# The opening of an attention and FNet kernel: another heads' table for the first batch, work moved to ScalarE and GpSimd, queues reordered

## The chip, the cores and the metric

The kernel runs on one core of one Trainium2 chip. A core has five engines with their own instruction queues: TensorE (PE, whose weight loads are listed apart as PEld), VectorE (DVE), ScalarE (ACT), GpSimd (POOL) and SyncE (SP), which here only issues DMAs. An engine works through its queue in order, and waits in front of an instruction until the semaphores that it needs are there. The metric is the time on the device in microseconds; less is better.

## The reference

Eight batches of 8 heads, 576 tokens and 64 columns a head, all in fp32. First linear attention, then a Fourier mix with an MLP:

```python
q_s = exp(q - max(q, -1)); q_s = q_s / (sum(q_s, -1) + 1e-9)       # softmax over the 64 columns
k_s = exp(k - max(k, 2));  k_s = k_s / (sum(k_s, 2) + 1e-9)        # softmax over the 576 tokens
kv  = einsum('bhsd,bhse->bhde', k_s, v)                            # 64 x 64 a head
x   = einsum('bhsd,bhde->bhse', q_s, kv)  -> (8, 576, 512)         # heads side by side
mixed = real(fft(fft(x, axis=1), axis=2))
u   = x + mixed
un  = (u - mean(u)) / sqrt(var(u) + 1e-6)
out = u + max(un @ w_ch1, 0) @ w_ch2                               # 512 -> 2048 -> 512
```

## The kernel before

The batches are worked one after the other. What this document is about is the opening, batch 0, up to its MLP; batches 1 and up, and the MLP of all of them, are not touched.

**Keys and the heads' table.** The keys come transposed, two heads to a block of 128 rows, so there are four blocks `k00` to `k03` (`first_keys`, from L541). For each: maximum on VectorE (L554), exponential on ScalarE with its sum (L557), four transposes on PE (`turn`, L562), a copy from PSUM on ScalarE (`four`, L565). The last 64 tokens of all blocks are turned together (`last`, L570) and copied by VectorE (`fifth`, L573). `inverse` (L576, L577) takes the reciprocal of the sums. The products with the values (`times`, L586) give one 64x64 block for each head; the two heads of a pair lie one above the other in 128 rows. `scale` (L589) multiplies them with the reciprocals while it copies them from PSUM into `self.pairs[0]`, 128 rows by four pairs by 65 columns; the 65th column is one, and gives the softmax's sum of a query when it is multiplied along.

**Queries.** Batch 0's 576 query rows are split into four tiles of 128 rows, A, B, C and D, whose rows mirror each other in time (so that sums and differences of them are the folded input of a real Fourier transform), and one tile t of the remaining rows (64 of batch 0 and 64 of batch 1). For each tile: maximum by head (L968, VectorE), subtraction (L973, GpSimd for A, B and C, VectorE for D and t), exponential (L977, ScalarE), transposes (L985, PE), a copy from PSUM (L996, or L1006 for t into `self.F`, both ScalarE). For A to D the product with the table is made in `own_times_kv` (L840): sixteen matmuls of 64 rows with 64x65 of the table, whose 65th columns are turned into reciprocals (L862, L864) and multiplied in while VectorE copies the result from PSUM into x (L876). Tile t is normalized before its product (L946, L947, L948, L957, VectorE); GpSimd folds its transposed columns (L1018 to L1026), and `t_times_kv` multiplies them (L840 and L1061): 24 matmuls. ScalarE copies the results out (L1070, L1073), and VectorE folds the tile `g` over columns (L1085, L1087, L1088).

**Folds and transform.** `folded(0)` gives four tiles `eo`: 0 and 1 are sums of x rows, 2 and 3 differences (`tokens`, L1104). `columns` folds them over the features (L1115 and L1116 for the sums, L1110 for the differences), and the differences are combined again (`by`, L1123; `again`, L1129 and L1130). PE multiplies them with cosine tables (`e0`, `e1`: L1217) and sine tables (`e2`, `e3`: L1224), adds g's part (`tails`, L1234); the result is copied out (L1246 to L1250), transformed over the features (L1264, L1267), added to x (L1281 to L1295) and normalized, transposed (L1365), and goes into the MLP, whose first product is L1467.

**What sets the order.** The engines' queues are filled by an order written by hand. `OPENING` is a string of keys and steps (`14.75 t inverse, 14.76 k0 scale`); the steps are issued in the order of the keys, which are no times. Each engine sees its own instructions in that order. `WARM` puts extra matmuls on PE, whose results are not used (key, number, columns; L270). `BY_ACT` names the query tiles whose product ScalarE copies out. The loads of the opening are issued on SyncE in one list (`loads_first`): four blocks of keys, tile t's rows in four loads (L296), two of query rows (L315), `shared_firsts` (L299: four single rows of t, 8 KB, into rows that one of the loads before writes), values (L310, L311), transform tables (L343 to L347), then the weights. PSUM's tiles `two` have three buffers in the opening and `tr` two, taken in turn.

Of the kernel before, what the change touches and what calls it, by code (L numbers as in the profile page):

```python
# [52 lines left out]
HD = D // 2  # L53
NN = HD + 1
# [36 lines left out]
7.25 k01 turn, 7.56 k02 exp, 7.75 k03 max, 8.32 k01 four, 8.51 k02 turn, 8.82 k03 exp, 8.90 A max, 9.50 B max,  # L91
9.58 k02 four, 9.65 A less, 9.77 k0 last, 10.10 k0 inverse, 10.27 k03 turn, 10.42 k0 fifth, 10.69 B less,
10.80 A exp, 11.30 k03 four, 11.84 B exp, 11.85 A turn, 12.20 C max, 12.45 A copy,
12.80 D max, 12.90 C less, 12.95 B turn, 13.00 t max, 13.10 D less, 13.20 t less, 13.55 B copy, 14.00 k00 kv, 14.01 k01 kv, 14.10 C exp, 14.11 C turn, 14.12 D exp, 14.13 t exp, 14.14 C copy,
14.2 k02 kv, 14.3 k03 kv, 14.4 D turn, 14.41 D copy, 14.75 t inverse, 14.76 k0 scale, 14.8 t normal, 15.0 A kv, 15.1 t turn, 15.31 t copy, 15.4 C kv, 15.45 B kv,
18.48 A inverse, 18.50 A out, 18.60 C inverse, 18.61 C out, 18.62 D kv, 18.90 B inverse, 19.01 B out,
19.63 D inverse, 19.70 D out, 20.00 t fold, 20.1 t join, 20.2 t kv, 20.3 t parts, 20.43 tokens0, 20.5 columns0, 20.6 e0,
20.70 tokens1, 20.80 columns1, 20.9 e1, 21.02 roots,
21.1 c0 hi, 21.11 c0 lo, 21.12 c1 hi, 21.13 c1 lo,
21.15 t folds, 21.2 tokens2, 21.3 tokens3, 21.35 columns2, 21.4 columns3, 21.5 by2, 21.6 by3, 21.7 again2, 21.75 e2, 21.76 kept0, 21.8 again3, 21.85 e3, 21.9 tails,  # L100
21.91 c0 shift, 21.92 c0 sign, 21.93 c0 add,
# [37 lines left out]
class _Block:  # L139
    def __init__(self, ctx, tc, q, kT, v, w1, w2, ft, cd, out):  # L140
# [134 lines left out]
    def loads_first(self, fetch):  # L275
# [37 lines left out]
        def queries(i):  # L313
# [4 lines left out]
        order = [lambda: nc.gpsimd.memset(v[0:64, 4, :], 0.0), table, *each(keys), shared, lambda: queries(0), lambda: queries(1),  # L318
                 shared_firsts, lambda: values(0), lambda: values(2), self.tables, *(lambda i=i: fetch(i) for i in range(11))]
        later = [step for _, step in self.keys_to(1) + [(0, self.prepare)] + self.values_to(1, 0)]  # L320
# [219 lines left out]
    def first_keys(self, b):  # L540
# [3 lines left out]
        v = [v[:, :, r * P:(r + 1) * P] for r in range(NR)]  # L544
        copy, box, top = nc.vector.tensor_copy, {}, {}
        rec = self.small.tile([P, NR], F32, tag="kinv", name="kinv", bufs=2)
        steps = {}

# [23 lines left out]
        def fifth():  # L572
            copy(self.fifth[64:], box["last"][64:])  # L573

        def inverse():
            V.tensor_scalar(out=rec[:], in0=rec[:], scalar1=ATT_EPS, scalar2=None, op0=ALU.add)  # L576
            V.reciprocal(rec[:], rec[:])  # L577

        def times(r):
# [20 lines left out]
    def opening(self, fetch, converted):  # L600
# [20 lines left out]
        named("t fold,t join", self.t_fold(shared))  # L621
        named("t kv,t parts,t folds", self.t_times_kv(0))
        for n, it in own.items():
            named(f"{n} max,{n} less,{n} exp", self.q_exp_spread(it, V if n == "D" else None))
            named(f"{n} turn,{n} copy", self.q_turn(it))
            named(f"{n} kv,{n} inverse,{n} out", self.own_times_kv(it, act=n in BY_ACT))
        for name, f in zip(("tokens", "columns", "by", "again"), self.folded(0)):
# [195 lines left out]
    def by_head(self, b, left, turned=False, n=DH + 1, shared=False):  # L823
# [24 lines left out]
        return [(r, t.rearrange("p h (r n) -> p h r n", n=n)) for r, t in parts] + [px]  # L848

    def own_times_kv(self, it, shared=False, act=False):  # L850
        nc, V, (_, b, c, u) = self.nc, self.nc.vector, it
# [179 lines left out]
    def q_times_kv(self, it, turned=False):  # L1031
# [12 lines left out]
        return [(0, times), (1.3, out)]  # L1044

    def t_times_kv(self, b):
        nc, V = self.nc, self.nc.vector
# [34 lines left out]

        def folds():
            g = self.live["g", b]
            V.scalar_tensor_tensor(out=g[:, 1:HD], in0=g[:, D - 1:HD:-1], scalar=self.sign[:, 0:1], in1=g[:, 1:HD],  # L1085
                                   op0=ALU.mult, op1=ALU.add)
            V.tensor_tensor(out=g[:, NN:NN + QD], in0=g[:, 0:QD], in1=g[:, HD:QD:-1], op=ALU.subtract)  # L1087
            V.tensor_tensor(out=g[:, 0:QD], in0=g[:, 0:QD], in1=g[:, HD:QD:-1], op=ALU.add)  # L1088

        return [(0, times), (1.3, copies), (8 if b > 1 else 3, folds)]  # L1090

    def folded(self, b):
# [5 lines left out]
        def tokens_folded(some):  # L1100
            for i in some:
                e, op = ((V if b < 2 else G), ALU.add) if i < 2 else (V, ALU.subtract)
                eo[i] = self.halves()
                e.tensor_tensor(out=eo[i][:, 0:D], in0=self.xpart(b, i % 2, 0), in1=self.xpart(b, i % 2, 1), op=op)  # L1104

        def columns_folded(some):
            for i in some:
                e, op = ((V if b < 2 else G), ALU.add) if i < 2 else (V, ALU.subtract)
                t = eo[i]
                e.tensor_tensor(out=t[:, 1:HD], in0=t[:, 1:HD], in1=t[:, D - 1:HD:-1], op=op)  # L1110
# [883 lines left out]
```

## Time and profile before

| | |
|---|---|
| median of 3 runs | 1006.84 us (1006.43 to 1006.99) |
| the profiled execution, span from the first to the last instruction | 1006.6 us |
| granted TensorE clock, mean | 1.000 |
| matmul busy / span | 995.6 us, 99% |
| VectorE, ScalarE, GpSimd busy | 71%, 49%, 44% |
| DMA moved | 236.37 MB, 235 GB/s |
| first product of batch 0's MLP (L1467) starts at | 42.70 us |

For the profiled execution no time other than its span is given. It stands 0.24 us below the median of the runs. A group in the profile is a source line, an engine and an operation with its tiles; `x8` behind it is a count. A matmul in fp32 shows as two records on PE and two weight loads on PEld, a transpose as one of each. "issue" in the chain is time in which an engine waited for nothing that the profile shows.

### The profile page before, as it was taken

Reading aid. Unit: us, or ns where it says so; the run is one execution under the profiler, and the core shown is the slowest. Engines: PE = TensorE matmul, PEld = TensorE weight load, DVE = VectorE, ACT = ScalarE, POOL = GpSimd, SP = SyncE. Lnnn points to the kernel's source line nnn. Section 1 sums busy time; section 2 is a strip of 40 time slices with the busy share of each in tenths; the row PEclk is TensorE's granted clock in tenths of the full one; section 3 lists DMA queues with packets and bytes.
Section 4 is the critical chain, followed back from the end, with each engine's and each line's share of the span. In section 5 each row is a group of like instructions: output and inputs, shape, how many; then the busy total and the mean of one; then the engine's idle time right before and its main releaser. Section 6 shows DMA issues by size and latency. Waiting matters only on the chain.

```text
span 1006.6 us, 19808 instructions
## 1 busy us (share of the span) xinstructions
PE 995.6 (99%) x7562; PEld 855.7 (85%) x7562; DVE 718.6 (71%) x1356; ACT 493.2 (49%) x1277; POOL 442.9 (44%) x445
## 2 busy tenths in 40 slices
PE   8999999999999999999999999999999999999998
PEld 6844464888888899889988998899889998998897
DVE  6898898666765887588756877688667945685563
ACT  4585642872468228832775177625772342151200
POOL 4263420357535637664655465655646450040000
PEclk9999999999999999999999999999999999999999
DMA  9987499687989666975677577847753765674573
GB/s 300 258 281 245 158 240 346 205 243 226 342 283 272 230 230 219 266 237 210 251 220 242 206 269 237 253 174 270 231 204 135 267 213 200 224 265 172 183 256 132
DMA packets 123559, 236.37 MB, mean 235 GB/s; under 512 B 24184, under 2 KB 88440, under 8 KB 112840
## 3 DMA queue, kind: packets, MB, share of 16 engines
q1 hardware_dynamic: 123096, 234.58, 71.0%
q8 instruction: 60, 0.98, 0.4%
q14 instruction: 35, 0.29, 0.1%
q10 hardware_dynamic: 288, 0.26, 0.1%
q0 software_dynamic: 80, 0.26, 0.1%
HBM read 199.94 MB, written 39.06 MB: 237 GB/s over the span
## 4 chain that ended last, share of the span: by engine, by line
PE 87%; DVE 7%; ACT 3%; DMA 1%; issue 1%; SPq 0%; POOL 0%; DVEq 0%; POOLq 0%
PE bb L1544 16%; PE ba L1544 11%; PE bc L1544 11%; PE bb L1671 10%; PE ba L1671 7%; PE bc L1671 7%; PE bb L1641 5%; PE bc L1479 2%; PE bb L1760 2%; PE two L840 2%; PE one L755 2%; PE two L1207 1%; PE two L1264 1%; PE ba L1479 1%; PE bc L1760 1%; PE ba L1760 1%
## 5 line engine op out<-in xcount | busy, mean ns | idle before, releaser
L1544 PE MATMUL bb<-unT,big 128*128 128x256 f32 x768 | 183.3, 380 | 0.0
L1544 PEld LDWEIGHTS bb<-unT,big 128*128 128x128 f32 x768 | 144.8, 190 | 20.7 <-DVE u L1514 0.7
L1556 ACT ACTIVATE big<-big 128x512 f32<-128x512 f32 x96 | 59.8, 629 | 147.6 <-DVE big L1555 141.0
L1544 PE MATMUL ba<-unT,big 128*128 128x256 f32 x512 | 123.9, 382 | 0.0
L1544 PE MATMUL bc<-unT,big 128*128 128x256 f32 x512 | 121.5, 380 | 0.1
L817 ACT ACTIVATE qT<-q 32x128 f32<-32x128 f32 x384 | 117.9, 307 | 5.9 <-DVE q L807 0.8
L1544 PEld LDWEIGHTS bc<-unT,big 128*128 128x128 f32 x512 | 96.9, 190 | 13.7 <-DVE big L1555 0.5
L1544 PEld LDWEIGHTS ba<-unT,big 128*128 128x128 f32 x512 | 95.5, 190 | 13.9 <-issue 0.5
L1514 DVE TENSOR_TENSOR u<-bb,s 128x512 f32<-128x512 f32 x66 | 45.2, 685 | 85.0 <-PE bb L1544 66.5
L1671 PE MATMUL bb<-big 128*128 128x128 f32 x848 | 103.8, 276 | 0.2 <-DVE u L1678 0.2
L1671 PEld LDWEIGHTS bb<-big 128*128 128x128 f32 x848 | 98.9, 192 | 1.0 <-DVE u L1678 1.0
L1390 POOL COPY unT<-unT 32x256 f32<-32x256 f32 x98 | 42.0, 428 | 90.2 <-DVE unT L1382 85.9
L1621 POOL TENSOR_TENSOR x<-x,big 128x512 f32<-128x512 f32 x45 | 60.9, 1368 | 46.0 <-DVE big L1678 19.7
L1617 DVE TENSOR_TENSOR big<-big 128x512 f32<-128x512 f32 x98 | 79.9, 842 | 0.0
L1671 PE MATMUL ba<-big 128*128 128x128 f32 x640 | 79.0, 276 | 0.0
L1671 PEld LDWEIGHTS ba<-big 128*128 128x128 f32 x640 | 75.0, 192 | 0.8
L1390 ACT COPY unT<-unT 32x256 f32<-32x256 f32 x126 | 50.7, 402 | 31.3 <-DVE unT L1382 29.5
L804 POOL TENSOR_TENSOR q<-q,qm 128x512 f32<-128x512 f32 x24 | 25.8, 1073 | 88.2 <-DVE qm L799 53.1
L405 POOL TENSOR_TENSOR big<-big 128x512 f32<-128x512 f32 x24 | 30.4, 1268 | 68.4 <-ACT big L1556 68.4
L1641 PE MATMUL bb<-big 128*128 128x256 f32 x256 | 58.3, 379 | 0.0
L1555 DVE TENSOR_TENSOR big<-bc,u 128x512 f32<-128x512 f32 x64 | 44.0, 688 | 17.3 <-PE bc L1544 16.4
L1641 PEld LDWEIGHTS bb<-big 128*128 128x128 f32 x256 | 48.0, 190 | 6.1
(336 smaller groups left out, 1917.9 us busy)
## 6 DMA issues: line engine op xcount, KB each, us to landing
big<-w2d SPq DMA_DIRECT2D x67, 1024.0 KB, 4.6
big<-w1s SPq DMA_DIRECT2D x64, 896.0 KB, 4.7
big<-w2s SPq DMA_DIRECT2D x16, 1024.0 KB, 4.8
big<-in_w_dram SPq DMA_DIRECT2D x21, 512.0 KB, 6.0
w2d<-big SPq DMA_DIRECT2D x42, 256.0 KB, 6.5
kb<-in_kT_dram SPq DMA_DIRECT2D x28, 320.0 KB, 7.8
q<-in_q_dram SPq DMA_DIRECT2D x28, 256.0 KB, 6.0
vt<-in_v_dram SPq DMA_DIRECT2D x84, 80.0 KB, 2.7
```

The lines of the kernel that those rows point to most:

```text
L405: e1.tensor_tensor(out=to(4), in0=at(2), in1=at(3), op=ALU.add)
L817: nc.scalar.activation(to[t, i * Q:i * Q + Q], one, ACT.Exp)
L1390: copy(to, of)
L1514: plus = lambda t: V.tensor_tensor(out=temp(t), in0=box["bb"][:], in1=box["s1"][:], op=ALU.add)
L1544: nc.tensor.matmul(bank()[:, i, :], lhsT=w[:, WA_AT[m], k * P:(k + 1) * P], rhs=self.unT[g][:, B_AT[m], k, :], start=first and i == 0 and ...
L1555: steps = [(0, lambda: V.tensor_tensor(out=hp(i), in0=bank()[:], in1=u()[:], op=ALU.add)), (0.8, lambda: nc.scalar.activation(hp(i), hp(i) ...
L1556: (0.8, lambda: nc.scalar.activation(hp(i), hp(i), ACT.Relu))]
L1617: e.tensor_tensor(out=to(o), in0=to(x), in1=to(y), op=op)
L1621: E.tensor_tensor(out=x, in0=x, in1=tile(m), op=ALU.add)
L1641: nc.tensor.matmul(box[name][:, i, :], lhsT=h[p][:, A_AT[m], i * P:(i + 1) * P], rhs=self.stream[n][:, p, :], start=p == 0 and (m != 1 or ...
L1671: nc.tensor.matmul(box[place[n]][:, i, :], lhsT=own(m)(A_AT[n])[:, f, :], rhs=w[:, r // 2, r % 2 * P:r % 2 * P + P], start=first and f == ...
L1760: nc.tensor.matmul(bank()[:, i, :], lhsT=h[p][:, A_AT[m], i * P:(i + 1) * P], rhs=w[:, p, :], start=first and i == 0 and p == 0, stop=p == ...
```

## The change

It touches batch 0 only, and has these parts:

- The heads' table of batch 0 becomes `self.diagonal`, 128 rows by four pairs by two heads by 65 columns, in which each pair's two 64x65 blocks stand on a diagonal and the rest is zero. It lies in a part of `w1sb` that is filled later. Four more fills on GpSimd set the columns of ones and zeros. `inverse` multiplies the reciprocals with these columns into `both` (128x8), so that `scale` writes both halves at once, 512 columns, zeros among them.
- A query tile is multiplied by four matmuls with all 128 rows and 130 columns (`first_times_kv`) in place of sixteen; tile t by four of 128x128 and four of 64x128 (`first_t_times_kv`) in place of 24.
- B's product is copied out and scaled by ScalarE, in eight activations of 64 columns. The copy `fifth` goes from VectorE to ScalarE.
- GpSimd makes the differences `tokens2`, `tokens3`, `columns2`, `columns3`, and g's folds (four operations in place of three), which VectorE made.
- The load of t's four first rows goes from SyncE's queue to ScalarE's, and is issued there behind the copy `k03 four`.
- `OPENING` is put into another order: on VectorE the inverse of the keys' sums ahead of A's maximum, and t's and D's maximum and subtraction ahead of the scale with t's normalization before it; on ScalarE t's exponential ahead of C's, and `kept0` (a copy of x) ahead of t's copies; on PE the turn of C between the value tables, A's and C's products first, then B's, D's and t's. One group of warm-up matmuls (key 18.63) is left out. GpSimd's fills of `vt` come behind t's folds.

```diff
-WARM = (2, 5, 256, 1), (6.5, 1, 256, 1), (7.26, 1, 64, 1), (8.52, 1, 64, 1), (10.5, 5, 256, 1), (18.63, 3, 256), (22.111, 10, 256)
+WARM = (2, 5, 256, 1), (6.5, 1, 256, 1), (7.26, 1, 64, 1), (8.52, 1, 64, 1), (10.5, 5, 256, 1), (22.111, 10, 256)
 OPENING = """
...
+7.25 k01 turn, 7.56 k02 exp, 7.75 k03 max, 8.32 k01 four, 8.51 k02 turn, 8.82 k03 exp, 8.84 k0 inverse, 8.90 A max, 9.50 B max,
+9.58 k02 four, 9.65 A less, 9.77 k0 last, 10.27 k03 turn, 10.3 k03 four, 10.4 t firsts, 10.42 k0 fifth, 10.43 C max, 10.69 B less,
+10.80 A exp, 11.80 C less, 11.84 B exp, 11.85 A turn, 12.20 t max, 12.25 t less, 12.3 D max, 12.4 D less, 12.5 t exp, 12.95 B turn, 13.1 C exp, 13.2 A copy,
+13.3 D exp, 13.4 B copy, 14.00 k00 kv, 14.01 k01 kv, 14.11 C turn, 14.14 C copy,
+14.2 k02 kv, 14.3 k03 kv, 14.4 t inverse, 14.5 t normal, 14.6 k0 scale, 14.7 t turn, 14.8 t copy, 15.0 A kv, 15.1 C kv, 15.2 D turn, 15.3 D copy, 15.45 B kv, 15.5 D kv, 15.6 t fold, 15.7 t join,
+18.48 A inverse, 18.50 A out, 18.60 C inverse, 18.61 C out, 18.90 B inverse, 19.01 B out, 19.02 kept0,
+19.2 tokens0, 19.25 tokens2, 19.3 columns0, 19.35 columns2, 19.4 D inverse, 19.45 D out, 19.5 tokens1, 19.55 columns1, 19.6 tokens3, 19.65 columns3,
+20.2 t kv, 20.3 t parts, 20.6 e0, 20.9 e1, 21.02 roots,
...
-BY_ACT, BY_DVE = "", (2, 3)
+BY_ACT, BY_DVE = "B", (2, 3)
...
+        n = 2 * (DH + 1)
+        self.diagonal = self.w1sb[:, 8:10, :].rearrange("p a n -> p (a n)")[:, 0:NR * n].rearrange("p (r h n) -> p r h n", r=NR, h=2)
+        for h in range(2):
+            for i in range(2):
+                nc.gpsimd.memset(self.diagonal[64 * i:64 * i + 64, :, h, DH:], float(h == i))
...
         def shared_firsts():
-            load(tail[0:P:Q], self.q[b:b + 2].rearrange("b s n -> (b s) n")[::S // 2])
+            nc.scalar.dma_start(tail[0:P:Q], self.q[b:b + 2].rearrange("b s n -> (b s) n")[::S // 2])
...
         def fifth():
-            copy(self.fifth[64:], box["last"][64:])
+            nc.scalar.copy(self.fifth[64:], box["last"][64:])
...
+            V.tensor_tensor(out=both[:], in0=self.diagonal[:, :, :, DH], in1=rec[:].unsqueeze(2).to_broadcast([P, NR, 2]), op=ALU.mult)
...
         def scale():
-            V.tensor_tensor(out=self.pairs[b][:, :, 0:DH], in0=box["kv"][:, :, 0:DH],
-                            in1=rec[:].unsqueeze(2).to_broadcast([P, NR, DH]), op=ALU.mult)
+            V.tensor_tensor(out=self.diagonal[:, :, :, 0:DH], in0=box["kv"][:, :, 0:DH].unsqueeze(2).to_broadcast([P, NR, 2, DH]),
+                            in1=both[:].unsqueeze(3).to_broadcast([P, NR, 2, DH]), op=ALU.mult)
...
+    def first_times_kv(self, it, act=False):
...
+            for r in range(NR):
+                nc.tensor.matmul(px[:, r // 2, r % 2 * 2 * n:(r % 2 + 1) * 2 * n], lhsT=q[:, r, :],
+                                 rhs=self.diagonal[:, r].rearrange("p h n -> p (h n)"), start=True, stop=True)
...
+            if act:
+                for a in range(2):
+                    for k in range(NR):
+                        nc.scalar.activation(x[:, a, k, :], px[:, a, k, 0:DH], ACT.Copy, scale=rec[:, a, k:k + 1])
+                return
...
+    def first_t_times_kv(self):
...
+            for r in range(NR):
+                nc.tensor.matmul(px[:, r // 2, r % 2 * P:(r % 2 + 1) * P], lhsT=self.F[:, 2 * r, 0:P], rhs=table(r), start=True, stop=True)
+            for a in range(2):
+                for i in range(2):
+                    nc.tensor.matmul(px[64 * i:64 * i + 64, a, HD:HD + P], lhsT=self.F[:, 2 * (2 * i + a), P:], rhs=table(2 * i + a),
+                                     start=True, stop=True)
...
+    def g_folds(self, b, e):
...
+            e.tensor_scalar(out=g[:, D - 1:HD:-1], in0=g[:, D - 1:HD:-1], scalar1=self.sign[:, 0:1], scalar2=None, op0=ALU.mult)
+            e.tensor_tensor(out=g[:, 1:HD], in0=g[:, 1:HD], in1=g[:, D - 1:HD:-1], op=ALU.add)
...
-                e, op = ((V if b < 2 else G), ALU.add) if i < 2 else (V, ALU.subtract)
+                e, op = ((V if b < 2 else G), ALU.add) if i < 2 else (V if b else G, ALU.subtract)
```

More of the change, by code (lines that the diff above doesn't have):

```diff
@@ L92 @@
[L92 to L95, printed above, removed]
@@ L318, in loads_first @@
         order = [lambda: nc.gpsimd.memset(v[0:64, 4, :], 0.0), table, *each(keys), shared, lambda: queries(0), lambda: queries(1),
-                 shared_firsts, lambda: values(0), lambda: values(2), self.tables, *(lambda i=i: fetch(i) for i in range(11))]
+                 lambda: values(0), lambda: values(2), self.tables, *(lambda i=i: fetch(i) for i in range(11))]
         later = [step for _, step in self.keys_to(1) + [(0, self.prepare)] + self.values_to(1, 0)]
@@ L544, in first_keys @@
         v = [v[:, :, r * P:(r + 1) * P] for r in range(NR)]
-        copy, box, top = nc.vector.tensor_copy, {}, {}
+        box, top = {}, {}
         rec = self.small.tile([P, NR], F32, tag="kinv", name="kinv", bufs=2)
+        both = self.small.tile([P, NR, 2], F32, tag="krec2", name="krec2", bufs=1)
         steps = {}
@@ L621, in opening @@
         named("t fold,t join", self.t_fold(shared))
-        named("t kv,t parts,t folds", self.t_times_kv(0))
+        named("t kv,t parts,t folds", self.first_t_times_kv())
         for n, it in own.items():
@@ L625, in opening @@
             named(f"{n} turn,{n} copy", self.q_turn(it))
-            named(f"{n} kv,{n} inverse,{n} out", self.own_times_kv(it, act=n in BY_ACT))
+            named(f"{n} kv,{n} inverse,{n} out", self.first_times_kv(it, act=n in BY_ACT))
+        steps["t firsts"] = self.shared_firsts
         for name, f in zip(("tokens", "columns", "by", "again"), self.folded(0)):
@@ new lines, in first_t_times_kv, with times, copies, early @@
+    def first_t_times_kv(self):
+        nc, G, box = self.nc, self.nc.gpsimd, []
+        table = lambda r: self.diagonal[:, r, :, 0:DH]
+        def times():
+            px = self.two()
+            for r in range(NR):
[4 more added lines that the diff above has]
+                                     start=True, stop=True)
+            box.append(px)
+        def copies():
+            g, px = self.live["g", 0], box.pop()
+            nc.scalar.copy(g[:, 0:D].rearrange("p (a n) -> p a n", a=2), px[:, :, 0:HD])
+            x = self.xshared(0)[0:W]
+            for i in range(2):
+                nc.scalar.copy(x[:, i * HD:(i + 1) * HD].rearrange("p (a n) -> p a n", a=2), px[64 * i:64 * i + 64, :, HD:HD + P])
+        def early():
+            self.live["g", 0] = self.halves()
+            copies()
+        return [(0, times), (1.3, early), (3, lambda: self.g_folds(0, G))]
@@ L1081, in copies @@
                                    box[2 + h][64 * i:64 * i + 64, HD:HD + 2 * DH].rearrange("p (a d) -> p a d", a=2))
[L1083 to L1090, printed above, removed]
+        return [(0, times), (1.3, copies), (8 if b > 1 else 3, lambda: self.g_folds(b, V))]
     def folded(self, b):
```

32 lines of the change are left out of this document (26 added, 6 removed).

## The prediction

> **What bounds the kernel now.** I read the page first. TensorE is the bound of the whole span:
>
> ```profile
> PE 995.6 (99%) x7562; PEld 855.7 (85%) x7562; DVE 718.6 (71%) x1356; ACT 493.2 (49%) x1277; POOL 442.9 (44%) x445
> ```
>
> Only 11.0 of 1006.6 us have no matmul, so the next view is the busy time by stretches (columns: length, then PE, PEld, DVE, ACT, POOL with their records, granted clock, DMA share, GB/s):
>
> ```profile
> 0.00:20.22 20.22, 18.15 (x219) 14.53 (x220) 12.23 (x24) 12.40 (x24) 8.45 (x26) 1.00 0.87 280
> 20.22:21.74 1.52, 0.00 (x1) 0.00 (x0) 0.97 (x3) 0.00 (x0) 1.52 (x5) 1.00 1.09 377
> 21.74:42.70 20.96, 18.98 (x226) 16.49 (x225) 18.32 (x50) 10.43 (x31) 6.64 (x9) 1.00 1.15 284
> 42.70:50.00 7.30, 7.30 (x38) 6.50 (x39) 5.72 (x12) 4.25 (x9) 1.72 (x2) 1.00 0.81 248
> ```
>
> The opening loses 2.07 + 1.52 + 1.98 = 5.57 us of PE. From 42.70, where the first product of batch 0's MLP stands, PE has no gap. All that the change touches lies before that point, so one rule makes the sum: **the end moves as the first MLP product moves, one to one.** Busy time before that point is no guide, since part of it is warm-up matmuls. The third view is therefore the chain that ended last, within the opening (start, length, what):
>
> ```profile
> 9.94 1.28 DVE qm L968 x2
> 11.22 0.57 DVE kinv L576
> ...
> 12.05 0.67 DVE big L573
> ...
> 18.16 0.70 PE two L840 x32
> ...
> 20.22 1.52 issue
> ...
> 31.32 1.22 PE two L1224 x8
> ...
> 42.70 1.97 PE ba L1467 x8
> ```
>
> The reader is to see the marks at which before and after are compared: the products of tile A (18.16), a stall of PE of 1.52 us that no semaphore explains, the sine products (31.32) and the MLP (42.70). Between the first rows and 18.16 the chain runs on VectorE and ScalarE through the softmax of the shared tile t and the scaling of the heads' table.
>
> **The change part by part.** The rows that carry the prices, from the timelines of PE, VectorE, GpSimd and ScalarE:
>
> ```profile
> 10.01 0.66 PE L562 MATMUL tr<-ident,big 128*128 128x128 f32 x4
> ...
> 22.72 1.56 PE L270 MATMUL tr<-pairs 128*128 128x256 f32 x6
> 24.21 0.69 PE L840 MATMUL two<-pairs,F 64*64 64x64 f32 x32
> 24.73 0.41 PE L1061 MATMUL two<-pairs,F 64*64 64x64 f32 x16
> ...
> 33.80 1.27 PE L1264 MATMUL tr<-cd,Z 128*128 128x128 f32 x8 [0.32 <-DVE Z L1246]
> ```
>
> ```profile
> 19.36 0.69 DVE L876 TENSOR_TENSOR x<-two,qrec 128x512 f32<-128x512 f32 x1
> ...
> 27.23 0.29 DVE L1087 TENSOR_TENSOR eo<-eo 128x128 f32<-128x128 f32 x1
> 27.56 0.29 DVE L1088 TENSOR_TENSOR eo<-eo 128x128 f32<-128x128 f32 x1
> 27.77 1.29 DVE L1104 TENSOR_TENSOR eo<-x 128x512 f32<-128x512 f32 x2
> 28.97 0.75 DVE L1110 TENSOR_TENSOR eo<-eo 128x255 f32<-128x255 f32 x2
> ```
>
> ```profile
> 22.03 0.66 POOL L1025 TENSOR_TENSOR F<-T 128x256 f32<-128x256 f32 x1
> ```
>
> ```profile
> 34.33 0.18 ACT L1249 ACTIVATE ZT<-two 128x32 f32<-128x32 f32 x1
> 34.41 0.16 ACT L1250 COPY ZT<-two 128x32 f32<-128x32 f32 x1
> ```
>
> *The load of t's first rows* (4 rows, 8 KB) leaves SyncE's queue, so the values, the transform tables and the weights behind it go out earlier. None of them ends a wait on the chain above: I count nothing, and if they crowd the DMA engines, it is the small load that pays. On ScalarE's queue it stands behind the copy of the fourth block of keys. The turn for that copy ends at 10.01 + 0.66 = 10.67; with a copy of about 0.6 the load goes out at 11.3. How long it flies, the trace of before doesn't show; the nearest rows of the view of DMA issues (last number: median us from issue to landing) are
>
> ```profile
> big<-in_q_dram SPq DMA_DIRECT2D x2, 512.0 KB, 5.5
> ...
> out_dram<-x ACTq DMA_DIRECT2D x2, 128.0 KB, 1.7
> ```
>
> The second is ScalarE's queue, late in the kernel; the first is the opening, at 64 times the size. I take 2.0, near the second, because the size is small, with something added for engines that are busy 0.87 to 1.09 of the time; the ends are 1.2 and 5.5. Landing: 13.3. Behind the maximum of t, which waits for it on VectorE, stand D's maximum and subtraction, t's normalization and the table's scale, and with these all products of the tiles.
>
> *The chain to A's products.* VectorE loses the copy L573 (0.67, to ScalarE, which has room there) and the wait inside L576 (0.57): the inverse goes ahead of A's maximum, and its added product of 128x8 costs some 0.2. So the maxima of A, B and C, 0.63 each, run from 10.15 to 12.05; then VectorE stands 1.3 until 13.3. From there: t's maximum 0.63; t's subtraction 0.65 (half of L1104 x2, the same shape and operands) and up to 0.3 behind GpSimd's subtraction for C; D's pair 1.3; t's sums and division at 0.69 each with two small steps, 1.8; the new scale writes 512 columns out of PSUM, 0.69 as L876, where 256 were written before. With gaps of 0.03 that is 18.8, against 18.16. **+0.6.** ScalarE takes t's exponential ahead of C's, so C's turn and behind it the value tables of the third and fourth pair come later too; I get 18.0 for their end, just under the scale.
>
> *Products of the four tiles.* Sixteen quadrant matmuls cost 0.70. Four full ones of 130 columns are eight records as in L1264 x8, whose 1.27 holds the drain of the last; starts are 0.112 apart, so 0.91. **+0.2 a tile, +0.8 in all.**
>
> *The stall.* PE had 219 + 220 records behind it when it stopped with nothing to wait for. In the trace of the DMA queues between 19.0 and 20.4 stands one 16 KB packet (1, 0.02 MB) of an instruction queue:
>
> ```profile
> q8 instruction: 1, 0.02, 3.9%
> ```
>
> I read the stall as PE waiting for instructions, which came late through engines at a share of 1.09. A tile's products fall from 16 to 4 matmuls, t's from 24 to 8, each with two records and two weight loads. So the 439th record now falls into the cosine products, at 28 to 29, with nearly 10 us more for the same fetch. **-1.5.** D's products then end at 22.9, where before they had ended at 22.72. The ends of this term: 0 and -1.5.
>
> The Trainium skill, page "Runtime: NRT & Kernel Launch", section "Instruction fetch mechanics", says that crossing a 16 KiB block of instructions is mostly hidden. By that rule the stall would be something else, could stay where it is, and the sum would be 1.5 us higher; the trace, with its 1.52 us and no other releaser, speaks against it.
>
> *t's products* stood behind the warm-ups L270 (1.56, now removed) until 24.21. Now they wait for a bank of PSUM that ScalarE frees: B's tile in eight activations 128x64, from 22.4. L1249 and L1250 start 0.08 apart at 32 columns; I take 0.13 at 64, so 1.1 with the last one's length; ends 0.08 and 0.18 each. Start 23.6: -0.6. Their price rises from 0.93 (24.21 to 25.14) to 1.8, two groups like L1264's. End 25.4: **+0.3** against before. With the cosine products, forty records at 0.126 for 144 columns, PE is through at 30.7.
>
> *Folds.* VectorE loses B's scale 0.69, differences 1.29 + 0.75, and g's folds, 0.29 + 0.29 and one of 255 columns, some 0.4: 3.7 in all. GpSimd gets eight operations from about 23, when it is through with t's folds and the fills of vt that were moved behind them: two of 512 columns at some 1.1, four of 255 at 0.66 as L1025, two of 128 at 0.45: 5.7. The cover are PE's five us of cosine products. VectorE keeps 4.4 of sums and later folds. Undisturbed, the last fold would be done by 29.5 and PE alone would set the sine products. Against that stand these rows (timeline of all engines):
>
> ```profile
> 105.73 1.21 POOL L973 TENSOR_TENSOR q<-q,qm 128x512 f32<-128x512 f32 x1 [1.67 <-DVE qm L968]
> ...
> 106.08 1.02 DVE L1087 TENSOR_TENSOR eo<-eo 128x128 f32<-128x128 f32 x1
> ```
>
> L1087, 0.29 above, takes 1.02 beside GpSimd and ends as it ends. So such operations of the two engines run one after the other: 5.7 + 4.4 = 10.1 from 21.5, where the sum over A's and C's rows can begin, with overlaps while VectorE reads PSUM and gaps while g is still to come. I take 31.0 for the last fold and 31.15 for the sine products, against 31.32: **-0.15.**
>
> The four fills of the table's ones lie on GpSimd at the start, before it has any data to work on: nothing. The copy of A's first rows moves ahead of t's copies on ScalarE, 0.6, and is done while PE still multiplies for t: nothing, unless t's products end before 24.5. From the sine products to 42.70 no step is changed.
>
> **Sum.** The first MLP product at 42.55 against 42.70. The profiled span, 1006.6, lies 0.24 under the median of the runs, 1006.84; so the forecast is **1006.7**. A measurement of this kernel can tell about 0.2%, 2.0 us, from no change.
>
> **Rivals.**
>
> *Within 2 us (the forecast).* For it: 1.5 of stall and 0.6 of warm-ups, gained, meet 0.6 before A's products, 0.8 in the tiles and 0.9 in t's, lost; the folds decide nothing by more than tenths. With a flight of 1.2 to 2.8 and the ends of the small terms: 1006.2 to 1007.8.
>
> *Slower: the small load is late.* Beyond a flight of about 1.8 everything slips with it, one to one: at 4.5 the first MLP product stands at 45.1, **1009.2**; from 4.0 it decides. For it: the share of 1.09 and the row of 5.5. Against it: 8 KB on a queue of its own.
>
> *Slower: the folds alternate worse.* If GpSimd's 255-column forms, one with a scalar and all with a reversed operand, take 1.0 and no overlap is left, the last fold comes at 33: the sine products 1.9 later, the weights' conversions on VectorE pushed against Z, **1009.0**. From a last fold at 31.2 it decides. The Trainium skill, page "SBUF — State Buffer", section "Who interferes with whom", has it that a VectorE instruction with two SBUF inputs and a GpSimd one that reads SBUF exclude each other for a whole instruction; the row at 106.08 agrees.
>
> *The stall only moves.* It costs 1.5 in the cosine products: **1008.2**. Against it: the fetch has 10 us more, and later fetches leave PE without a gap between 42.70 and 50.00.
>
> *Faster: what is removed passes whole.* A's products at 18.2 (the load in at 12.7), the stall and the warm-ups gone, 2.1, and folds that are never last: **1004.7**. Against it: t's products still wait for B's eviction, and are 0.9 longer.
>
> **How the numbers follow.** Forecast 0.46, late load 0.18, alternation 0.12, moved stall 0.06, faster 0.18. Slower by over 0.2%: the late load, half of the alternation and the upper tails, 0.28. Faster by over 0.2%: 0.18, all of that case. Within: 0.54. The range of 1004.6 to 1009.2 leaves out half of the late load, part of the alternation and a tail of the faster case; the forecast's own is 1006.2 to 1007.8.
>
> **What would show it.** Right: no idle of PE near 1.5 at the old place; t's maximum starting at 13.0 to 13.6; A's products at 18.6 to 19.0, each tile 0.9; eight activations in 1.1; VectorE's 0.29 folds stretched to 0.6 to 1.2 beside GpSimd; the first MLP product at 42.2 to 43.3. Wrong: t's maximum after 15, an idle of PE of over 1 us within the cosine products, a last fold after 32, or a way from the first MLP product to the end that differs from 963.9 by over half a us.

## The result, and the profile after

The changed kernel takes 1013.41 us (median of 4 runs, 1012.92 to 1014.03) against 1006.75 (4 runs, 1006.43 to 1006.99): **1.0066 of the time before, 95% interval 1.0052 to 1.0081, 6.7 us slower.** The forecast was 1006.7 in a range of 1004.6 to 1009.2.

The first section of the profile after:

```profile
PE 996.9 (99%) x7428; PEld 858.0 (85%) x7428; DVE 718.3 (71%) x1348; ACT 496.0 (49%) x1286; POOL 451.9 (45%) x457
```

Its span is 1011.2, the first product of batch 0's MLP (now line 1541) starts at 47.42, and 963.7 us follow. Before, it started at 42.70 with 963.9 to follow: in these two profiles all of the loss lies in the opening. The stretches of the opening:

```profile
10.00:12.50 2.50, 2.49 (x14) 1.88 (x11) 1.28 (x2) 1.17 (x2) 0.52 (x1) 1.00 1.07 379
12.50:15.00 2.50, 0.92 (x6) 0.69 (x7) 0.69 (x1) 1.26 (x2) 2.50 (x3) 1.00 1.06 338
15.00:17.50 2.50, 2.46 (x44) 2.11 (x42) 1.12 (x2) 0.00 (x0) 0.02 (x1) 0.64 1.04 381
17.50:20.00 2.50, 0.36 (x2) 0.39 (x3) 2.40 (x6) 2.19 (x5) 0.00 (x0) 0.50 1.08 373
20.00:22.50 2.50, 2.50 (x38) 2.17 (x38) 0.80 (x2) 1.14 (x3) 0.00 (x0) 0.50 1.07 377
```

PE idles from 12.5 to 15 and from 17.5 to 20, and from 15 on it runs at half of its clock (the value behind POOL's, 0.64 and 0.50), which no stretch of before did. What it waits for stands in the timelines of ScalarE's queue, VectorE and PE (the first two lines are the kernel before: the same load on SyncE's queue, and the maxima of C, D and t):

```profile
8.69 0.70 SPq L299 DMA_DIRECT2D big<-in_q_dram  x1
...
12.75 1.87 DVE L968 TENSOR_REDUCE qm<-big 128x8 f32<-128x512 f32 x3
```

```profile
10.53 1.11 ACTq L304 DMA_DIRECT2D big<-in_q_dram  x1
```

```profile
11.15 1.28 DVE L1037 TENSOR_REDUCE qm<-big 128x8 f32<-128x512 f32 x2 [1.31 <-DMA big<-in_q_dram]
12.64 0.69 DVE L1037 TENSOR_REDUCE qm<-big 128x8 f32<-128x512 f32 x1 [0.21 <-DMA big<-in_q_dram]
16.34 0.69 DVE L1037 TENSOR_REDUCE qm<-big 128x8 f32<-128x512 f32 x1 [3.02 <-DMA ft<-in_ft_dram]
```

```profile
19.64 1.09 PE L1054 MATMUL tr<-ident,big 128*128 128x128 f32 x4 [2.18 <-issue]
...
23.66 2.06 PE L868 MATMUL two<-big 128*128 128x130 f32 x16 [0.21 <-DVE big L598]
...
29.44 1.13 PE L899 MATMUL two<-big,F 128*128 128x128 f32 x8 [1.39 <-POOL eo L1178]
```

ScalarE starts to give out the load of t's first rows at 10.53. The last semaphore update of that load in the trace is at 16.16: 5.6 us of flight for 8 KB. The last of the maxima, t's, starts at 16.34 (the named table load is not its input; the first rows are). Before, the load was in at 11.13 and t's maximum, the last of three from 12.75, started at 13.94, so nothing waited for it. A's maximum starts at 11.15, where it was 9.94. A's products start at 23.66 instead of 18.16, and t's at 29.44 instead of 24.21.

One warning on the base line. In every run since, the time exceeds the span by 1.7 to 1.9 us, so the profiled execution of before, with a span of 1006.6, was a long one, of some 1008.4: that is why the spans differ by 4.6 and the medians by 6.7. Spans of the kernel before run from 1004.0 to 1007.5. A second profile of it, further down, has 41.85 for the MLP. Differences of two profiles are therefore good to 1 us or so, and the verdicts below rest on the timed runs; each experiment is compared with the kernel before on the same chip.

### The profile page after: what moved, and what is told of

The parts are those of the page before. It is cut to its first block, busy times and chain, and to the rows that moved or that the text cites. A ratio compares the mean times of both kernels' runs of the same rounds, so it can differ in the third digit from the quotient of the medians.

```text
span 1011.2 us, 19556 instructions
## 1 busy us (share of the span) xinstructions
PE 996.9 (99%) x7428; PEld 858.0 (85%) x7428; DVE 718.3 (71%) x1348; ACT 496.0 (49%) x1286; POOL 451.9 (45%) x457
## 4 chain that ended last, share of the span: by engine, by line
PE 84%; DVE 6%; ACT 5%; issue 2%; POOL 2%; DMA 1%; SPq 0%; POOLq 0%; ACTq 0%; DVEq 0%
PE bb L1618 15%; PE ba L1618 10%; PE bb L1745 10%; PE bc L1618 10%; PE ba L1745 7%; PE bc L1745 7%; PE bb L1715 5%; PE bc L1553 2%; ACT qT L827 2%; PE two L1281 1%; PE two L1338 1%; PE one L765 1%; PE two L850 1%; PE bb L1834 1%; PE ba L1553 1%
```

## The experiments

All results in one table; the difference is that of the medians on one chip, with the interval of the ratio. The ratio isn't that of the medians, so the two can differ by half a us or more (b1, b4). The last column is one execution each.

| kernel | what | us | less before | 95% of the ratio | first MLP product |
|---|---|---|---|---|---|
| changed | | 1013.41 | +6.7 | 1.0052 to 1.0081 | 47.42 |
| a1 | changed, load back on SyncE | 1009.29 | +2.0 | 1.0007 to 1.0027 | 44.80 |
| b1 | before, load on ScalarE | 1012.82 | +5.6 | 1.0031 to 1.0068 | 45.91 |
| c1 | changed, SyncE held as before | 1014.16 | +7.2 | 1.0053 to 1.0080 | 48.08 |
| c2 | changed, more warm-ups | 1012.38 | +5.5 | 1.0039 to 1.0070 | 46.10 |
| b2 | before, ten more records | 1007.45 | +0.2 | 0.9992 to 1.0016 | 42.89 |
| a2 | a1, folds on VectorE | 1009.14 | +1.9 | 1.0009 to 1.0030 | 45.28 |
| a4 | a1, inverse later | 1009.19 | +2.2 | 1.0015 to 1.0033 | 43.71 |
| a5 | a4, B on VectorE | 1010.54 | +3.6 | 1.0021 to 1.0048 | 44.99 |
| b3 | before, diagonal table alone | 1009.45 | +2.5 | 1.0016 to 1.0034 | 43.45 |
| b4 | before, new order alone | 1010.31 | +3.3 | 1.0016 to 1.0037 | 45.11 |
| a7 | a4, kept0 later | 1009.30 | +2.4 | 1.0013 to 1.0031 | 43.66 |
| a8 | a4, A's copy ahead | 1008.63 | +1.8 | 1.0008 to 1.0026 | 43.19 |
| a6 | a4, five repairs | 1007.84 | +1.0 | 1.0001 to 1.0026 | 42.68 |
| c3 | a6, differences on VectorE | 1007.72 | +0.8 | 0.9997 to 1.0015 | 42.48 |
| d1 | before, three small moves | 1007.60 | +0.7 | 0.9996 to 1.0014 | 43.30 |

### The load, undone and done alone

Theory L: the move of the 8 KB load is the whole loss. Theory F: the load is half, the folds and B's activations the rest.

```diff
a1  (changed kernel)
-            nc.scalar.dma_start(tail[0:P:Q], ...)
+            load(tail[0:P:Q], ...)                 # SyncE, ahead of the values again
b1  (kernel before)
-            load(tail[0:P:Q], ...)
+            nc.scalar.dma_start(tail[0:P:Q], ...)  # behind k03 four
```

> The changed kernel with one part undone: t's four first rows are loaded on SyncE's queue again, in their old place ahead of the values. Theory L (the load's move is the whole loss): query tile A lands at 9.9 again, t's maximum starts by 12.2 instead of 16.3, the first MLP product stands at 42 to 43.3 instead of 47.4, time 1006 to 1007.5. Theory F (the load costs only about half, the folds on GpSimd and B's eight activations the rest): first MLP product at 44.5 or later, time 1008.5 to 1010. The part of the loss that lies outside the span (6.7 us of time against 4.6 us of span) goes away too if ScalarE's early DMA causes it, and stays at about 1.5 if it does not.

> The kernel before with that one part done: t's four first rows on ScalarE's queue, issued behind the copy of the fourth keys' block (12.9 us, since that copy stands behind A's exponential here). Theory L: query tile A lands 1.2 later, the load flies 4 to 6 us, t's maximum starts at 17 to 18 instead of 13, the first MLP product stands 4 to 5 later, time 1010.5 to 1013. Theory F: the load is in by 15, time 1007.5 to 1009.5.

Both agree on the load: undoing it takes 1.0066 down to 1.0017, 4.9 us, and doing it alone costs 1.0050, 5.0 us (by medians 4.7 and 5.6). In b1 the load is given out at 12.49 and t's maximum starts at 17.59 (VectorE's timeline):

```profile
13.31 1.28 DVE L971 TENSOR_REDUCE qm<-big 128x8 f32<-128x512 f32 x2
17.59 0.69 DVE L971 TENSOR_REDUCE qm<-big 128x8 f32<-128x512 f32 x1 [2.99 <-DMA ft<-in_ft_dram]
```

But a1 is not back at before: 2 us remain. b1's time lies where theory L had it, a1's where theory F had it, so neither is right as a whole: the load is some three quarters. What F named for the rest, the folds and B's activations, is tested further down (a2, a5), and neither shows as a loss there.

### What of the load costs: the flight, the queries, the clock

Three things stand in the profile after the move: the load flies for 5.6 us, the query tiles come late (A's maximum at 11.15), and PE's clock falls while it waits.

```diff
c1  (changed kernel): row 0 on SyncE in the old place, three rows on ScalarE
+            load(tail[0:1], ...)
-            nc.scalar.dma_start(tail[0:P:Q], ...)
+            nc.scalar.dma_start(tail[Q:P:Q], ...)
c2  (changed kernel)
-... (10.5, 5, 256, 1), (22.111, 10, 256)
+... (10.5, 8, 256, 1), (14.05, 9, 256, 1), (22.111, 10, 256)
```

> The changed kernel, with one of the four rows loaded on SyncE in the old place, so that SyncE is held again before the values, and the three others on ScalarE's queue as in the change. This keeps the values behind the query tiles. Query tile A lands at 9.8 to 10.2 instead of 11.1. If the three rows wait behind the values that were issued ahead of them, they still fly 4 to 6 us from 10.5 and t's maximum starts at 14.5 to 16.5: time 1011 to 1013. If the released values were the whole trouble, the rows are in by 13 and the time is 1009 to 1010.

> The changed kernel with more warm-up matmuls where PE stands idle: eight in place of five ahead of A's turn, and nine ahead of C's turn. In the changed kernel PE's granted clock is 0.64, 0.50 and 0.50 from 15 to 22.5, and the value tables of the third and fourth pair take 2.1 us instead of 1.4. If the clock is a cost on the path, it stays at 1.0 here, these tables take 1.4, and the time is 0.7 to 1.2 under the changed kernel's 1013.4. If it is no cost, the same time.

In c1 the queries are nearly in time, and it helps nothing:

```profile
10.44 1.93 DVE L1040 TENSOR_REDUCE qm<-big 128x8 f32<-128x512 f32 x3 [0.72 <-DMA big<-in_q_dram]
16.09 0.69 DVE L1040 TENSOR_REDUCE qm<-big 128x8 f32<-128x512 f32 x1 [3.72 <-DMA big<-in_q_dram]
```

So it is the load's own flight: given out at 10.38, last update 15.87, and t's maximum at 16.09. The values were given out on SyncE between 7.4 and 9.7, ahead of it, and were in at 15.18. In the kernel before, SyncE holds the load until t's other rows are in, at 8.60, and gives out the values behind it; so it flew 2.4 us (issued 8.69, last update 11.13). That the query tiles come late because of the values is not shown: c2 has the changed kernel's order on SyncE, and its first maximum starts at 9.51. In c2 PE's clock stays up:

```profile
15.00:17.50 2.50, 2.50 (x35) 2.23 (x32) 1.93 (x3) 0.52 (x1) 0.00 (x0) 1.00 1.07 376
17.50:20.00 2.50, 2.50 (x15) 2.19 (x13) 2.36 (x6) 2.22 (x5) 0.00 (x0) 1.00 1.09 378
20.00:22.50 2.50, 2.29 (x48) 1.82 (x47) 0.73 (x2) 0.90 (x2) 0.00 (x0) 1.00 1.09 386
```

The value tables of the third and fourth pair take 1.4 us again instead of 2.2. PE's timeline gives the price, from the turn of C to the products of A:

```profile
19.65 0.60 PE L1054 MATMUL tr<-ident,big 128*128 128x128 f32 x4
...
22.36 2.06 PE L868 MATMUL two<-big 128*128 128x130 f32 x16 [0.21 <-DVE big L598]
```

The turn starts where it did in the changed kernel (19.64), and the products 1.30 earlier (23.66 there). All of that is the clock: the turn and the tables take 1.9 instead of 3.2 us. The maximum of t started 0.80 earlier in c2, but the added warm-ups held the turn until 19.65. In time the gain, 1.0055 where the changed kernel has 1.0066, is about 1 us as expected, but the intervals overlap: likely, not shown.

### The stall of PE

```diff
b2  (kernel before)
-(10.5, 5, 256, 1)
+(10.5, 10, 128, 1)
```

> The kernel before with the fourth group of warm-ups cut into ten matmuls of 128 columns in place of five of 256: the same PE time, ten more records of matmul and ten of weight load. If the stall of 1.52 us at 20.22 is PE waiting for its own instructions, it moves to some 20 records earlier in the order of the work (within the products of tile A or C) and keeps 1 to 2.5 us; time 1006 to 1008. If it hangs on the work at that place, it stays at C's 10th matmul, 219 + 20 records in.

Three timelines of PE, of the kernel before, of the same in a second profile, and of b2:

```profile
19.37 0.85 PE L840 MATMUL two<-pairs,big 64*64 64x65 f32 x41
21.74 1.04 PE L840 MATMUL two<-pairs,big 64*64 64x65 f32 x55 [1.52 <-issue]
```

> The kernel before, unchanged, profiled once more. The profiled run of before had a span of 1006.6, while its runs since have spans of 1004.0 to 1007.5 about a median of 1005.3 (time less 1.75). If the difference lies in the opening, the first MLP product is at 41 to 42 here and the stall of PE is shorter than 1.52; if it lies behind the opening, the first MLP product is at 42.5 to 43 again.

```profile
19.49 0.85 PE L840 MATMUL two<-pairs,big 64*64 64x65 f32 x41
20.90 1.04 PE L840 MATMUL two<-pairs,big 64*64 64x65 f32 x55 [0.56 <-issue]
...
41.85 1.97 PE L1467 MATMUL ba<-unT,big 128*128 128x256 f32 x8 [0.88 <-ACT eo L1326]
```

```profile
19.78 0.69 PE L840 MATMUL two<-pairs,big 64*64 64x65 f32 x31
21.25 1.17 PE L840 MATMUL two<-pairs,big 64*64 64x65 f32 x65 [0.78 <-issue]
```

Twice the stall stands behind the 41st record of this group, and ten more matmul records ahead of it put it behind the 31st; each time it is behind 219 matmul records and 220 weight loads in all. It hangs on the count of instructions, not on the work: PE waits for its own instructions. (I had expected 20 records earlier; it is the ten that were added. The length, 0.78, is under the 1 to 2.5 that I had expected.) The trace of DMA packets agrees. In these three, and in d1 and b4, which come further down and stall one record later, a 16 KB packet of the instruction queue starts at 19.28, 18.64, 18.91, 19.88 and 20.08, and PE goes on 2.2 to 2.5 us behind that start. So the length depends on how early PE arrives and how late the packet: 1.52, 0.56, 0.78, 1.31, 1.75. The changed kernel has no stall at this place or at this count. The mechanism held; of the 1.5 that I had booked, the two profiles of the kernel before leave between 0.56 and 1.52, and which is usual isn't shown.

### What remains without the load: 2 us

In a1 the product that `inverse` now makes waits for the first rows, and holds A's maximum behind it; a4 puts it where it was.

```diff
a4  (a1)
-8.84 k0 inverse, 8.90 A max, 9.50 B max, ...
+8.90 A max, 9.50 B max, ... 10.10 k0 inverse,
a2  (a1)
-(V if b else G, ALU.subtract)   ... self.g_folds(0, G)
+(V, ALU.subtract)               ... self.g_folds(0, self.nc.vector)
a5  (a4)
-BY_ACT, BY_DVE = "B", (2, 3)
+BY_ACT, BY_DVE = "", (2, 3)
```

> As a1_sp_firsts, with the inverse of the keys' sums behind the maxima of A and B on VectorE, its place before the change. In a1 the added 128x8 product stood from 9.31 to 11.60 and held A's maximum: its program order puts it behind the first rows' load, whose rows it need not have. If that wait is what is left of the loss, A's maximum starts at 9.5, the first MLP product 1 to 1.7 earlier than a1's and the time is 1007 to 1008.2 (a1: 1009.3). If the rest is elsewhere (PE's clock, products, B's activations), the time stays at 1008.7 to 1009.5.

> As a1_sp_firsts, and the differences (tokens 2 and 3, columns 2 and 3) and g's folds on VectorE again. If GpSimd and VectorE only take turns there, the sine products start within 0.5 us of a1's and the time is a1's within 0.7; if GpSimd is slower than what it relieves, a2 is 1 to 2 us faster than a1; if it relieves VectorE, a2 is 1 to 2.5 us slower.

> As a4_inverse_later, and B's product copied out by VectorE in one operation, in place of eight activations that took 1.75 us with t's products behind them. If these are on the path, the first MLP product is 0.5 to 1 earlier than a4's; if VectorE's extra 0.69 is on the path instead, 0 to 0.7 later.

a4 gains nothing that can be told from a1 (1.0024 and 1.0017), though its first MLP product stands 1.1 earlier in the profile; in its new place the small product takes 0.69 beside GpSimd's subtractions instead of 0.17. a2 can't be told from a1: in both, PE goes into the sine products without a gap (33.47 and 33.99), so that the folds are not what it waits for there. a5 is 1.4 slower than a4 on the same chip, though the intervals of their ratios touch: ScalarE's copy of B is likely a gain, with its eight activations at 1.75 us, not 1.1.

```diff
b3  (kernel before): self.diagonal, both, first_times_kv, first_t_times_kv; all else as before
b4  (kernel before): OPENING and WARM of the changed kernel without `t firsts`; all else as before
```

> The kernel before with the diagonal table alone: order, queues, folds, warm-ups and evictions as before. From the traces so far a tile's product takes 1.03 instead of 0.70, t's 1.7 instead of 0.93, the scale 0.69 instead of 0.42, and the fetch stall of 1.5 at 20.2 goes. Sum: +0.3 +1.3 +0.8 -1.5, less what the warm-ups before t's products absorb: first MLP product 0 to 1.2 later than before, time 1007 to 1008.5 beside 1007.3. If the stall only moves: 1008.5 to 1010.

> The kernel before with the new order of the steps alone (and the warm-ups of key 18.63 left out): the first rows' load on SyncE, small products, folds and all evictions on VectorE as before. If the order by itself costs (t's exponential ahead of C's and of A's copy, so that PE waits and its clock falls), the time is 1 to 2 above before, and the granted clock falls under 1 between 15 and 20; if it is neutral, within 0.7 of before.

Each alone costs about as much as both with the rest of the change: by the ratios 2.5 and 2.7 us, against 2.4 for a4, with intervals that cover each other. So the parts do not add up, and why is not shown. b3 lost its stall, as expected, and was slower than expected all the same. In b4 the clock stayed at 1.00 until 25 and fell behind that (0.83 from 25 to 30), not between 15 and 20, and the stall of PE took 1.75. Where a4 loses, its waits of PE say:

```profile
PE tr L1053 <- issue: 1.5, 1, 1.5
PE two L898 <- POOL eo L1177: 1.4, 1, 1.4
```

The first is the turn of C. It needs the PSUM buffer that the copy of A's transposes frees, and on ScalarE that copy stands behind the exponentials of t and C. The second is t's products; the named fold is not their input.

```diff
a8  (a4)
-12.5 t exp, 12.95 B turn, 13.1 C exp, 13.2 A copy,
+12.45 A copy, 12.5 t exp, 12.95 B turn, 13.1 C exp,
a7  (a4)
-19.01 B out, 19.02 kept0,   ...   21.75 e2,
+19.01 B out,                ...   21.75 e2, 21.76 kept0,
a6  (a4): both; C's turn behind the value tables, the inverse ahead of A's maximum
     without the added product (that moves into the scale), the scale ahead of t's division
```

> As a4_inverse_later, with the copy of A's transposes ahead of t's exponential on ScalarE. In a4 it stands behind the exponentials of t and C, frees its PSUM buffer at 17.1, and PE waits from 15.65 to 17.20 to turn C, with the value tables behind. If that is on the path, the turn of C starts at 15.4 to 16.2, the products of A at 18.9 to 19.4 instead of 19.94, time 0.5 to 1 lower than a4's: 1008.2 to 1008.7. If t's normalization and the scale bind anyway: 1009.

> As a4_inverse_later, with the copy kept0 back in its old place behind the cosine products. It takes a PSUM buffer; with three of them in turn, t's products get the buffer that B's eight activations have to free (a4: PE idle 24.33 to 25.71) when kept0 stands ahead of them, and C's buffer, free at 23.3, when it does not. If so, t's products start 1.2 to 1.4 earlier than in a4 and the time falls by 0.7 to 1.4, to 1007.8 to 1008.5. If GpSimd's folds of t or its differences hold t's products, nothing changes: 1009.2.

> As a4_inverse_later, with both of these, the turn of C behind all value tables, the inverse ahead of A's maximum without the added product (that moves to the scale), and the scale ahead of t's division. By the sum of the traces: products of A at 17.6 to 18.2, t's products at 22.5 to 23.5, first MLP product 2 to 3 earlier than a4's; time 1006 to 1007, at or under before. If the losses overlap, 1007.5 to 1008.5.

a8 lies some 0.5 below a4, as expected, but the intervals overlap; its turn of C comes at 16.68 instead of 17.20 and waits for C's own exponential there. a7 shows the buffer. `kept0` takes one of the three PSUM buffers; moved ahead of t's products, it gives these the buffer that B's activations free. Back in its place, t's products start at once (PE's timeline of a7):

```profile
24.12 1.05 PE L898 MATMUL two<-big,F 128*128 128x128 f32 x8
...
29.09 0.51 PE L1290 MATMUL two<-big,eo 128*128 128x144 f32 x2 [0.42 <-DVE eo L1188]
...
32.11 1.40 PE L1297 MATMUL two<-ft,eo 128*128 128x144 f32 x8 [0.30 <-DVE eo L1203]
```

1.6 earlier than in a4 (25.71), but the time is the same: now the cosine and sine products wait for folds. VectorE and GpSimd take turns there, and GpSimd's operations are longer than I had them (a6, VectorE's and GpSimd's timelines; the row at 26.83 takes 0.28 when it runs alone):

```profile
26.21 0.70 DVE L1188 TENSOR_TENSOR eo<-eo 128x128 f32<-128x128 f32 x1
26.83 1.35 DVE L1189 TENSOR_TENSOR eo<-eo 128x127 f32<-128x127 f32 x1
```

```profile
26.73 1.31 POOL L1177 TENSOR_TENSOR eo<-x 128x512 f32<-128x512 f32 x1
28.11 0.72 POOL L1183 TENSOR_TENSOR eo<-eo 128x255 f32<-128x255 f32 x1
28.82 1.21 POOL L1118 TENSOR_SCALAR eo<-eo,sign 128x255 f32<-128x255 f32 x1
```

a6 gets 1.2 of the 2.2 back by medians (the intervals of a4 and a6 overlap; which of the five repairs counts is not separated) and still has 0.66 us of PE waiting for the last fold:

```profile
31.13 1.40 PE L1297 MATMUL two<-ft,eo 128*128 128x144 f32 x8 [0.66 <-DVE eo L1203]
```

```diff
c3  (a6): tokens2, tokens3, columns2, columns3 on VectorE, g's folds alone on GpSimd
d1  (kernel before)
-8.82 k03 exp, 8.90 A max, ... 10.10 k0 inverse, 10.27 k03 turn, 10.42 k0 fifth, ... 11.30 k03 four,
+8.82 k03 exp, 8.84 k0 inverse, 8.90 A max, ... 10.27 k03 turn, 10.3 k03 four, 10.42 k0 fifth,   (fifth on ScalarE)
```

> As a6_all, with the differences (tokens 2 and 3, columns 2 and 3) on VectorE again and only g's folds on GpSimd. In a6 the sine products wait 0.7 us for the last fold, which follows GpSimd's differences and alternates with them. VectorE has 2.0 more to do and loses fewer waits: last fold between 30.7 and 31.7 (a6: 31.65), time between 0.9 under a6 and equal: 1007 to 1007.9.

> The kernel before with three small moves out of the change: the inverse of the keys' sums ahead of A's maximum, the copy fifth on ScalarE, and the copy of the fourth keys' block ahead of A's exponential. VectorE saves 0.7 and a held instruction of 0.6 ahead of t's maximum; the scale is then bound by the value tables, so that A's products come 0.3 to 0.6 earlier. The stall of PE ends when its instructions arrive, at 21 to 21.7, whatever comes before it, and may take the gain: time between 0.6 under before and equal.

Neither can be told from the kernel before, or from a6. No version was found that beats it. In d1's profile the moves won nothing ahead of the stall: A's rows came 1 us later than before (its maximum at 10.97), and A's products started at 18.92 instead of 18.16. The stall then lasted until 22.35:

```profile
22.35 1.04 PE L840 MATMUL two<-pairs,big 64*64 64x65 f32 x54 [1.31 <-issue]
```

## Why the prediction was wrong, point by point

- *The end moves as the first MLP product, one to one.* Right for the change: +4.72 there, +4.6 in the span. It is no exact rule: over all profiles 962.7 (b2) to 966.1 us (b1) follow that product, so b1's 45.91 hides 2 us of its loss.
- *The base.* I set a span of 1006.6 beside a median time of 1006.84 as if they were alike. Time is 1.7 to 1.9 more than span, so the profile that all my rows came from was an execution some 1.6 us longer than the median.
- *"How long it flies ... I take 2.0, near the second, because the size is small."* This is the step that failed. It flew 5.6 (5.1 from issue to use in b1, 5.7 in c1). Its small size did not save it. By the landing times it came in among the last of what SyncE had given out ahead of it, and the same edit had just released the values to go ahead; no run holds the values back behind a load on ScalarE's queue, so that reason is read from the traces and not shown by an edit. The flight lies just over my upper end of 5.5; I had put the value near the wrong row, that of a quiet stretch. With 5.6, my own sum from 10.5 gives t's maximum at 16.1, and 16.34 was measured.
- *"None of them ends a wait ... I count nothing."* The released transfers are the ones that the load came in behind, so to count nothing for them was wrong. A's maximum was 1.2 late as well, but c2, with the same order on SyncE, has it at 9.51, so that is no fixed price; and c1, where it is 0.7 earlier, is no faster.
- *Rival "the small load is late", 1009.2, chance 0.18.* The right rival, with place and mechanism, but priced for a flight of 4.5 and without PE's clock. That PE's clock halves in such a wait stood in no row of before, and I left it out; by c2's timeline it cost 1.3 ahead of A's products.
- *The stall, -1.5.* Its cause and its going were right; its size was taken from one execution, and the other profile of the kernel before has 0.56.
- *A tile at 0.91, "+0.2 a tile, +0.8 in all".* The new price is right: two tiles start 1.90 ahead of the next turn (23.66 to 25.56), 0.95 each. The old one was too high: 0.70 held the end of the last matmul, while A's products were followed by the next turn after 0.64, and the other three took 0.85 + 1.04 together, 0.63 each. So it is +0.3 a tile and +1.3 in all, and this term is short by 0.5.
- *"The copy of A's first rows moves ahead ... nothing."* Wrong: it took t's products' buffer, a wait of PE of 1.4 in a4; I had the wait for B, but not that the copy makes it. Taking it back alone (a7) gained no time, since the folds were next.
- *B's activations 1.1, the added product 0.2, GpSimd's 255-column form with a scalar 0.66.* Measured 1.75, 0.17 to 0.69, 1.21.
- *A's products at +0.6.* With the load in time (a4) they are at 19.94, +1.8: I had the value tables done at 18.0, and they are done at 19.15, since C's turn in front of them starts only at 17.20.
- *Folds: -0.15 by alternation.* The alternation is there (1.40 for 0.29 at the first cosine fold); in the changed kernel it is hidden, since PE comes to the sine products without a wait, and folds end waits of PE in a7 and a6, where other losses are repaired.

The sum of all terms, forecast at -0.15, is +2.0 to +2.2 without the load's move, by a1 and a4; the move brings the other 4.7 to 4.9. Of the 2.0, the terms above name the late value tables and the tiles; how the rest divides stays open.

## What to carry to other kernels

When a small load is moved to another queue, look at what its old place held back: here the transfers that were released went ahead of it, and it landed among the last of them. A row from a quiet stretch says little of a flight in a full one. A copy that is hidden in time can still make others wait, by the PSUM buffer that it takes in a rotation.

## What the runs showed of the hardware

A load of four rows, 8 KB, on ScalarE's queue landed 4.9 to 5.6 us after the start of its issue, with SyncE's loads on their way: 5.6 in the changed kernel, 4.9 in b1, 5.1 in c2, and 5.5 in c1 with three rows. On SyncE's queue, given out ahead of the values, it took 2.4 in the kernel before and 3.7 in a1. In the changed kernel 1.7 MB had been given out ahead of it: the values, 1.1 MB, with the last update at 16.02, and a transform table of 578 KB, at 17.43; the load's was at 16.16. In b1 the values were in at 15.42, and the load landed at 17.41, between a table given out ahead of it (16.74) and two more (17.53 and 17.91).

The trace of DMA packets divides the flight. In the changed kernel the issue took from 10.53 to 11.64, the four rows' packets started between 13.98 and 15.28, and the last update came at 16.16. In b1, c1 and c2 too the first packet came 2.4 to 2.9 us after the end of the issue. The Trainium skill, page "DMA: Bandwidth & Descriptors", section "Queues, rings and completion order", says that a DMA engine takes turns between the queues that have work, a packet at a time. The trace agrees in that the load's packets move while the table given out ahead of it has not landed (15.29 to 17.43), but these 2.3 us and more come first, and no run shows what they are. The issue took 1.11 us on ScalarE, 0.37 for the same engine's issue late in the kernel before.

PE's granted clock fell to 0.50 in the changed kernel after 12.5 to 15, a stretch with 0.92 of 2.50 us busy and no single wait of more than 1.25 us ahead of the fall; with warm-up matmuls in that stretch and the next (c2) it stayed at 1.00. The same matmuls (16 records of 64 columns) then took 1.07 to 1.12 instead of 0.64 to 0.69.

PE waited 0.56 to 1.75 us for instructions at a fixed count of them, while the DMA engines were full; how long differs from execution to execution. Whether that is part of the kernel's spread of 3.5 us is not shown: the two profiles of the kernel before differ by 0.96 in the stall and by 0.5 in the span.
